# First head pair's queries and keys: loaded token by token in four transfers and turned by TensorE, instead of loaded in 32-column blocks by eight transfers and turned by VectorE

## The chip, the cores and the metric

The kernel runs on one core of one Trainium2 chip. The metric is the device time of one execution in microseconds. Before the change the median of three runs is 948.99 us (948.95 to 949.15).

## The reference: what is computed

Routing attention over 4 batches, 8 heads, 768 tokens and head size 64, followed by a feed-forward block on 3072 tokens. Each query and each key is assigned to one of 16 centroids of its head, and a query sees only the keys of its own cluster:

```python
q_assign = np.argmax(np.einsum('bhsd,hcd->bhsc', q_n, c_n), axis=-1)
k_assign = np.argmax(np.einsum('bhsd,hcd->bhsc', k_n, c_n), axis=-1)
mask = q_assign[:, :, :, None] == k_assign[:, :, None, :]
scores = np.where(mask, scale * np.matmul(q, k.transpose(0, 1, 3, 2)), -1e9)
attn = softmax(scores)
x = np.matmul(attn, v)
h = x @ w_in
g = h * erf(softplus(h))
out = g @ w_out
```

All inputs and the output are float32. The weights are 512 x 2048 and 2048 x 512.

## The kernel before, in words

The attention part works on 16 pairs of heads (one batch, two heads that lie on the two halves of the 128 partitions). For each pair it needs the queries and keys with the head dimension on the partitions and the 768 tokens along the free axis: `qT` and `kT`, 128 x 768 float32. From these it computes, in this order: the similarities to the 32 centroid columns of the two heads (`similarities`, four TensorE products into the bank `turned[1]`, one each for a half of the queries and a half of the keys); the choice of the best centroid (`choose`: a VectorE transposition `sims`, a maximum, a comparison `hot`, a transposition `hotT`); one-hot mask rows for queries and keys (`masks`, bf16 tiles `qm`, `km`); bf16 copies of queries and keys (`vectors`: ScalarE writes `qv`, `kv`); the maximum of each query's scores (`maxima_step`, six of them for a pair, into `nmx`); and then the scores, exponentials, sums and products with `v`, in periods that interleave one pair's attention with the next pair's preparation (`period`, and lines 1541 to 1543). The feed-forward part comes after all pairs.

The change touches the start of the program, where the first pair cannot hide behind another one.

**Loading.** `load` (line 221) brings queries or keys of a pair as four transfers each, one for a head and a block of 32 columns of the head dimension. The tile `in_q` or `in_k` is 128 x 24 x 32: partition `e*64 + g*32 + t` holds token `t` of each of 24 token blocks, with 32 columns of head `e`. A run of memory is 32 floats, 128 bytes, and a transfer of 96 KB has 768 of them. So `qT` comes out of one VectorE transposition of 32 x 32 blocks over 128 x 768. `load_qk(p)` (line 244) does both for pair `p`. Pair 0 and pairs from 2 on use the pool `stage`, which has one buffer a name; pair 1 uses the memory of `x_more` (line 167). Transfers go out on the list `queues` (line 216), SyncE and ScalarE; after pair 0's (line 256) both entries are SyncE's. Line 251 loads the centroids, lines 253 and 255 pair 0, line 257 pair 1, line 1501 pair 2; pair 0's `v` and the first blocks of the weight `w_in` follow on SyncE (lines 1524 to 1526).

**Order.** `te`, `ve`, `ae`, `ge` and `sy` are the five engines, wrapped so that each keeps the program's order (line 119). While the first loads are under way, TensorE executes products that nobody reads: `warm(n, into, rhs)` issues `n` bf16 products with the identity as the stationary operand. Before the change there are 17 of them on 256 columns (line 1487), then the transposition of the normalised centroids `cn` into `pct` (line 1489), then 3 more on 384 columns. VectorE normalises the centroids (lines 356 to 371; `twice` is an intermediate of the square root), then transposes `qT` (line 1493), copies the turned centroids into `ccT` (two copies, one for each half of the partitions), and transposes `kT` (line 1499). `similarities(0)`, `vectors(0, ...)`, `products(0)` (the first score products, into a `sc` buffer of the two in the pool `ps_s`) and `warm(9, ...)` follow, then `choose(0)`.

**Names of PSUM tiles.** `wide` has two banks, used here for the maxima; `also` is the other buffer of `ps_s` (line 1513), used in turn with `wide` by the six first maxima; `turned[0]` and `turned[1]` are one bank each. `HW` is 384, half of the tokens; `HJ` is 3, the 128-token tiles of a half.

Of the kernel before, what the change touches and what calls it, by code (L numbers as in the profile page):

```python
# [9 lines left out]
F32 = mybir.dt.float32  # L10
# [9 lines left out]
P = 128  # L20
B, H, S, D = 4, 8, 768, 64
C = 16
NJ = S // P
Q = 32
NB = S // Q
HW = S // 2
QW = HW // 2
TW = QW + 1
HJ = NJ // 2
# [106 lines left out]
def kernel(  # L136
# [13 lines left out]
    te, ve, ae, ge = (  # L150
        InOrder(tc, e, in_order) for e in (nc.tensor, nc.vector, nc.scalar, nc.gpsimd)
    )
# [8 lines left out]
    turned = [ps.tile([P, 512], F32, name=f"turned{i}") for i in range(2)]  # L161
# [5 lines left out]
    x_more = const.tile([P, 3, HK, HT], F32, name="x_more")  # L167
# [6 lines left out]
    def passing(name, bufs, **kw):  # L174
        return attention.enter_context(tc.tile_pool(name=name, bufs=bufs, **kw))

    ps_s = passing("ps_s", 2, space=PSUM)
    wide = passing("ps_w", 1, space=PSUM).tile([P, 2, 512], F32, name="wide")

    const = passing("fixed", 1)  # L180
    stage = passing("stage", 1)
# [4 lines left out]
    ident = const.tile([P, P], F32, name="ident")  # L186
    identb = const.tile([P, P], BF16, name="identb")
    first = const.tile([P, P], BF16, name="first")
    pick = const.tile([P, 2, P], BF16, name="pick")
# [18 lines left out]
    rows = [{nm: const.tile([P, S], F32, name=f"{nm}T{i}") for nm in "qk"} for i in range(2)]  # L208
# [5 lines left out]
    pairs = {}  # L214
    sy = InOrder(tc, nc.sync, in_order)
    queues = [sy, ae]

    def heads(p):
        return p // HP, 2 * (p % HP)

    def load(p, nm, src, pl):
        if p >= NPAIR:
            return
        b, h0 = heads(p)
        if nm == "v":
            t = pl.tile([P, NJ, 2, D], F32, name="in_v")
            for e in range(2):
                queues[0].dma_start(out=t[:, :, e], in_=src[b, h0 + e].rearrange("(j p) d -> p j d", p=P))
        else:

            if pl is None:
                t = x_more.rearrange("p a k t -> p (a k t)")[:, (nm == "k") * S : (1 + (nm == "k")) * S]
                t = t.rearrange("p (n t) -> p n t", t=Q)
            else:
                t = pl.tile([P, NB, Q], F32, name="in_" + nm)
            for e in range(2):
                for g in range(D // Q):
                    queues[e if nm == "q" else e * g].dma_start(
                        out=t[e * D + g * Q : e * D + (g + 1) * Q],
                        in_=src[b, h0 + e, :, g * Q : (g + 1) * Q].rearrange("(n t) d -> t n d", t=Q),  # L240
                    )
        pairs.setdefault(p, {})[nm] = t

    def load_qk(p):
        load(p, "q", q, stage if p != 1 else None)
        load(p, "k", k, stage if p != 1 else None)
# [3 lines left out]
    cen = setup[:, 0:D]  # L250
    sy.dma_start(out=cen, in_=centroids.rearrange("h c d -> (h c) d"))

    load(0, "q", q, stage)
    tc.keep_in_program_order(nc.scalar.preload_act_table_set("natural_log_exp_and_others"))
    load(0, "k", k, stage)
    queues[1] = sy
    load_qk(1)

    make_identity(nc, ident)
    ve.memset(ccT, 0.0)  # L260
# [4 lines left out]
    for base, pattern, sign, op, fill in (  # L265
# [5 lines left out]
            out=first, in_=first, compare_op=op, fill=fill, base=base, pattern=pattern,  # L271
# [78 lines left out]
    def scalar_tile():  # L350
        n = next(spare)
        return setup[:, n : n + 1]
# [10 lines left out]
    ve.reciprocal(out=inv, in_=norm)  # L363
    twice = scalar_tile()
    ve.scalar_tensor_tensor(out=twice, in0=ss, scalar=inv, in1=norm, op0=ALU.mult, op1=ALU.add)
    norm = scalar_tile()
    ve.tensor_scalar(out=norm, in0=twice, scalar1=0.5, scalar2=1e-6, op0=ALU.mult, op1=ALU.add)
    rden = scalar_tile()
# [164 lines left out]
    def products(u):  # L533
        p, half, j = units[u]
        if u in sc_of:
            return
        st = pairs[p]
        sc = sc_of[u] = ps_s.tile([P, 2, 512], F32, name="sc", tag="s")
        for e in range(2):
            r = slice(e * D, (e + 1) * D)  # L540
            te.matmul(
                sc[:, e, 0:HW], lhsT=st["kT"][r, j * P : (j + 1) * P],
                rhs=st["qT"][r, half * HW : (half + 1) * HW], start=True, stop=False,
            )
# [937 lines left out]
    def warm(n, bank, rhs):  # L1482
        for _ in range(n):
            te.matmul(bank[:, 0 : rhs.shape[-1]], lhsT=identb, rhs=rhs, start=True, stop=True)

    zeros = lowest[1].rearrange("p t n -> p (t n)")
    warm(17, turned[1], pick.rearrange("p h n -> p (h n)"))
    pct = turned[0][:, 0:P]
    te.transpose(out=pct, in_=cn.rearrange("p e d -> p (e d)"), identity=ident)
    warm(3, turned[1], zeros)  # L1490
    st = pairs[0]
    st["qT"], st["kT"] = rows[0]["q"], rows[0]["k"]
    ve.transpose(out=st["qT"], in_=st.pop("q").rearrange("p n t -> p (n t)"))
    for e in range(2):
        ve.tensor_copy(
            out=ccT[e * D : (e + 1) * D, :, e * C : (e + 1) * C],
            in_=pct[e * D : (e + 1) * D].rearrange("d (r e c) -> d r e c", e=2, c=C)[:, :, e],
        )
    ve.transpose(out=st["kT"], in_=st.pop("k").rearrange("p n t -> p (n t)"))
    st.update(lows[0])  # L1500
    load_qk(2)
    similarities(0)
# [2 lines left out]
    for r in (0, D):  # L1505
        for half in range(2):
            for e in range(2):
                c = r + half * Q + e * C
                ve.tensor_copy(
                    out=pick[r : r + D, half, e * D : (e + 1) * D].rearrange("p (n c) -> p n c", n=2)[:, :, 1 : C + 1],  # L1510
                    in_=first[r : r + D, c : c + C].unsqueeze(1).to_broadcast([D, 2, C]),
                )
    also = ps_s.tile([P, 2, 512], F32, name="sc", tag="s")
    products(0)
    warm(9, turned[0], zeros)
    run(choose(0))
# [132 lines left out]
```

## Time and profile before

| | |
|---|---|
| median of three runs | 948.99 us (948.95 to 949.15) |
| the profiled execution's own time | 948.84 us |
| its span, first to last instruction | 947.1 us |
| outside the span | 1.74 us |
| TensorE busy | 938.7 us, 99% of the span |
| VectorE busy | 783.4 us, 83% |
| ScalarE busy | 546.9 us, 58% |
| GpSimd busy | 505.3 us, 53% |

The engines are called PE (TensorE products), PEld (its weight loads), DVE (VectorE), ACT (ScalarE), POOL (GpSimd) and SP (SyncE); a `q` behind the name is the engine's sequencer, which waits and issues transfers. The **chain of waits** is followed back from the last instruction: at each step to what released it, or to the instruction before it on its engine; its rows are a start in us, a duration in us, and what ran. The **timeline** lists instructions in order of time, neighbours of one kind merged: start, duration of the merged stretch, engine, line, operation, what is written and read, sizes, count, and in brackets the engine's idle time before it and what ended it. The view of **groups** gives for each kind of instruction its count, the busy time and the mean of one in ns. The view of **transfers** gives, for a stretch of time, the packets that the transfer engines moved, and their rate. Nearly all instructions carry line 127, that of the wrapper, so rows are told apart by the tiles they name. A product's record includes its way through the array, so records of neighbouring products overlap; what one costs in a row of many is the distance between starts.

### The profile page before, as it was taken

To read this page: it belongs to the slowest core of one execution; us is meant where nothing else is said; L and a number is where in the kernel's file an instruction comes from. 1 tells how busy PE (TensorE), PEld (TensorE's weight loads), DVE (VectorE), ACT (ScalarE), POOL (GpSimd) and SP (SyncE) were. 2 spreads that over 40 slices of the span, in tenths; PEclk is the share of its full clock that TensorE was granted. 3 is DMA by queue.
4 is the path that set the end of the run, shared out by engine and by line. 5 is a ranking of instruction groups with operands and counts; after the bars stand their busy time and mean duration, and the time that the engine had idled before them with its cause. 6 is when DMAs were issued, how large, how long until landed. Compare 5 with 4: busy or idle time off the path is not lost.

```text
span 947.1 us, 22315 instructions
## 1 busy us (share of the span) xinstructions
PE 938.7 (99%) x8756; PEld 707.0 (75%) x8756; DVE 783.4 (83%) x1416; ACT 546.9 (58%) x809; POOL 505.3 (53%) x357
## 2 busy tenths in 40 slices
PE   8999999999999999999999999999999999999998
PEld 3555555555555555588888888998999899989987
DVE  8888888888888887869886688688868977897887
ACT  3777777777777776476523543653257236525541
POOL 2688888888888888899119111460063016103600
PEclk9999999999999999999999999999999999999999
DMA  9354454444443621133885247353454436343533
GB/s 211 78 114 113 112 113 112 111 113 111 113 113 67 157 58 36 26 120 125 214 244 229 89 122 213 110 179 111 157 165 136 133 118 207 116 151 123 158 111 111
DMA packets 176344, 123.17 MB, mean 130 GB/s; under 512 B 132592, under 2 KB 143344, under 8 KB 176240
## 3 DMA queue, kind: packets, MB, share of 16 engines
q1 hardware_dynamic: 171872, 116.34, 43.2%
q0 software_dynamic: 1872, 4.98, 3.0%
q8 instruction: 69, 1.13, 0.5%
q10 hardware_dynamic: 2496, 0.43, 0.2%
q14 instruction: 35, 0.29, 0.1%
HBM read 91.78 MB, written 23.33 MB: 122 GB/s over the span
## 4 chain that ended last, share of the span: by engine, by line
PE 97%; DVE 1%; POOL 1%; DMA 0%; SPq 0%; ACT 0%; issue 0%; DVEq 0%; POOLq 0%
PE bank L127 43%; PE turned L127 31%; PE sc L127 17%; PE wide L127 6%; POOL more_out L127 1%; DVE nmx L127 1%; DMA in_k<-in_k_dram 0%; SPq L127 0%; DVE kT L127 0%; ACT qm L127 0%; ACT pr L127 0%; DVE sims L127 0%; ACT km L127 0%; DVE hotT L127 0%; DVE wide L127 0%
## 5 line engine op out<-in xcount | busy, mean ns | idle before, releaser
L127 POOL TENSOR_TENSOR more_out<-more_out,pr 128x768 f32<-128x768 f32 x128 | 217.6, 1700 | 17.1 <-ACT pr L127 7.5
L127 DVE TENSOR_REDUCE nmx<-wide 128x2 f32<-128x512 f32 (+2 forms) x189 | 179.1, 948 | 47.1 <-PE wide L127 46.1
L127 ACT ACTIVATE pr<-sc 128x768 f32<-128x768 f32 x192 | 148.4, 810 | 81.1 <-PE wide L127 73.2
L127 PE MATMUL turned<-pr,in_v 128*32 128x193 f32 x3072 | 145.2, 330 | 0.0
L127 POOL TENSOR_TENSOR g<-g 128x512 f32<-128x512 f32 x36 | 47.1, 1308 | 180.8 <-DVE g L127 178.8
L127 PEld LDWEIGHTS turned<-pr,in_v 128*32 128x32 f32 x3072 | 90.2, 109 | 51.3 <-issue 26.9
L127 DVE TENSOR_TENSOR g<-g 128x512 f32<-128x512 f32 x132 | 90.7, 687 | 23.0 <-PE bank L127 12.2
L127 PE MATMUL sc<-qT,kT 64*128 64x384 f32 x528 | 98.5, 485 | 0.0
L127 DVE TENSOR_TENSOR g<-bank,g 128x256 f32<-128x256 f32 (+1 forms) x128 | 64.6, 531 | 18.3 <-PE bank L127 9.5
L127 PE MATMUL bank<-g_more,g 128*128 128x256 f32 x320 | 75.7, 379 | 0.0
L127 PE MATMUL bank<-x_own,w_in 128*128 128x128 f32 (+1 forms) x440 | 74.0, 309 | 0.0
L127 ACT ACTIVATE a_s<-g 128x1024 f32<-128x1024 f32 x38 | 39.6, 1055 | 58.7 <-POOL g L127 45.9
L127 POOL TENSOR_TENSOR more_out<-pr,pr 128x768 f32<-128x768 f32 x32 | 59.2, 1849 | 19.7 <-ACT pr L127 19.6
L127 PEld LDWEIGHTS bank<-g_more,g 128*128 128x128 f32 x320 | 60.7, 190 | 8.6 <-DVE g L127 0.3
L127 DVE TENSOR_TENSOR g<-a_s,g 128x512 f32<-128x512 f32 x76 | 66.2, 892 | 0.8 <-ACT a_s L127 0.8
L127 PEld LDWEIGHTS bank<-x_own,w_in 128*128 128x128 f32 x440 | 63.2, 191 | 4.4 <-issue 0.6
L127 PE MATMUL wide<-kv,qv 64*128 64x256 bf16 (+2 forms) x378 | 64.8, 327 | 0.9 <-ACT km L127 0.6
L127 PE MATMUL bank<-w_out,g 128*128 128x256 f32 x280 | 64.5, 379 | 0.0
L127 PEld LDWEIGHTS <-qv 64*128 64x128 bf16 x384 | 23.1, 93 | 52.7 <-issue 37.8
L127 PE MATMUL wide<-km,qm 64*128 64x256 bf16 (+4 forms) x378 | 62.2, 326 | 0.0
L127 ACT ACT_TABLE_LOAD x40 | 51.3, 1283 | 17.7 <-DVE g L127 17.1
L127 PEld LDWEIGHTS sc<-qT,kT 64*128 64x128 f32 x528 | 46.3, 187 | 19.0 <-issue 2.0
(240 smaller groups left out, 1988.0 us busy)
## 6 DMA issues: line engine op xcount, KB each, us to landing
g_more<-b_dram SPq DMA_DIRECT2D x52, 512.0 KB
g_more<-w_dram SPq DMA_DIRECT2D x84, 256.0 KB
x_own<-in_moe_w_in_dram SPq DMA_DIRECT2D x13, 512.0 KB
in_v<-in_v_dram SPq DMA_DIRECT2D x32, 192.0 KB
x_dram<-more_out SPq DMA_DIRECT2D x128, 48.0 KB
x_own<-x_dram SPq DMA_DIRECT2D x6, 1024.0 KB
in_k<-in_k_dram SPq DMA_DIRECT2D x59, 96.0 KB
in_q<-in_q_dram SPq DMA_DIRECT2D x58, 96.0 KB
```

Of the source, the lines that this page charges most:

```text
L127: ins = getattr(self.engine, name)(*args, **kw)
```

## The change

The first pair no longer goes through `load`. For queries and for keys, a tile of the same `stage` buffer is filled by two transfers, one a head: partition `p` holds the tokens `j*128 + p` for six values of `j`, each with 64 floats of head 0 and 64 of head 1. Head 0 goes out on SyncE, head 1 on ScalarE; a transfer has 192 KB in 768 runs of 256 bytes. Pair 1's loads move from line 257 to a place behind the VectorE instruction `twice`; a VectorE memset of one column of `x_more` stands ahead of them, which all of its query transfers overwrite, so that they wait for it.

The turning is done by TensorE: a 128 x 128 block (128 tokens by two heads' 64 columns) is a single transposition, six for the queries (into `wide`) and six for the keys (into `also`, which is now taken earlier). Four copies out of PSUM, each 128 x 384 float32, replace the two VectorE transpositions: ScalarE copies the first halves, VectorE the second halves. The 17 warming products become 8, and the 3 behind `pct` are gone; `pct` now stands between the two halves of the keys.

```diff
-    load(0, "q", q, stage)
+    lying = {}
+    for nm, src in (("q", q), ("k", k)):
+        t = stage.tile([P, NB, Q], F32, name="in_" + nm).rearrange("p n t -> p (n t)")
+        lying[nm] = t.rearrange("p (j e d) -> p j e d", e=2, d=D)
+        for e in range(2):
+            queues[e].dma_start(out=lying[nm][:, :, e], in_=src[0, e].rearrange("(j p) d -> p j d", p=P))
     tc.keep_in_program_order(nc.scalar.preload_act_table_set("natural_log_exp_and_others"))
-    load(0, "k", k, stage)
+    pairs[0] = {}
     queues[1] = sy
-    load_qk(1)
...
     ve.scalar_tensor_tensor(out=twice, in0=ss, scalar=inv, in1=norm, op0=ALU.mult, op1=ALU.add)
+    ve.memset(x_more[:, 0, 0, 0:1], 0.0)
+    load_qk(1)
...
-    warm(17, turned[1], pick.rearrange("p h n -> p (h n)"))
+    warm(8, turned[1], pick.rearrange("p h n -> p (h n)"))
+    also = ps_s.tile([P, 2, 512], F32, name="sc", tag="s")
+    st = pairs[0]
+    st["qT"], st["kT"] = rows[0]["q"], rows[0]["k"]
+
+    def turned_whole(nm, bank, half):
+        for n in range(HJ):
+            te.transpose(
+                out=bank[:, half, n * P : (n + 1) * P],
+                in_=lying[nm][:, half * HJ + n].rearrange("p e d -> p (e d)"), identity=ident,
+            )
+        return bank[:, half, 0:HW]
+
+    to_q = [turned_whole("q", wide, half) for half in range(2)]
+    to_k = [turned_whole("k", also, 0)]
     pct = turned[0][:, 0:P]
     te.transpose(out=pct, in_=cn.rearrange("p e d -> p (e d)"), identity=ident)
-    warm(3, turned[1], zeros)
-    st = pairs[0]
-    st["qT"], st["kT"] = rows[0]["q"], rows[0]["k"]
-    ve.transpose(out=st["qT"], in_=st.pop("q").rearrange("p n t -> p (n t)"))
+    to_k.append(turned_whole("k", also, 1))
+    ae.copy(out=st["qT"][:, 0:HW], in_=to_q[0])
+    ve.tensor_copy(out=st["qT"][:, HW:], in_=to_q[1])
+    ae.copy(out=st["kT"][:, 0:HW], in_=to_k[0])
     for e in range(2):
         ve.tensor_copy(
             out=ccT[e * D : (e + 1) * D, :, e * C : (e + 1) * C],
             in_=pct[e * D : (e + 1) * D].rearrange("d (r e c) -> d r e c", e=2, c=C)[:, :, e],
         )
-    ve.transpose(out=st["kT"], in_=st.pop("k").rearrange("p n t -> p (n t)"))
+    ve.tensor_copy(out=st["kT"][:, HW:], in_=to_k[1])
...
-    also = ps_s.tile([P, 2, 512], F32, name="sc", tag="s")
     products(0)
```

## The prediction

> **What bounds the kernel now.** I read first the page (which engine fills the span), then the chain of waits over the first 12 us, then the timeline of the same stretch, then the transfers.
>
> ```profile
> PE 938.7 (99%) x8756; PEld 707.0 (75%) x8756; DVE 783.4 (83%) x1416; ACT 546.9 (58%) x809; POOL 505.3 (53%) x357
> ...
> PE 97%; DVE 1%; POOL 1%; DMA 0%; SPq 0%; ACT 0%; issue 0%; DVEq 0%; POOLq 0%
> ```
>
> Over the whole span TensorE is the bound: it is busy 99% and makes 97% of the chain. What ends sooner ahead of that long stretch ends the program sooner by the same amount, unless something else is due there. The start is different:
>
> ```profile
> 2.28 0.53 SPq L127
> ...
> 3.42 3.21 DMA in_k<-in_k_dram
> 6.64 0.02 issue
> 6.66 0.99 DVE kT L127
> 7.65 0.04 issue
> 7.69 0.86 PE turned L127 x4
> 8.55 0.02 issue
> 8.58 0.59 DVE sims L127
> ...
> 11.40 0.59 ACT km L127
> ```
>
> SyncE issues one key transfer after the other, the last lands at 6.64, VectorE turns `kT`, TensorE makes the similarities, and `sims` starts at 8.58. From there to the mask rows at 11.40 the chain runs through choices and masks that the change leaves alone. So its worth is read at one place: when does `sims` start, 8.58 now? Round it the timeline has:
>
> ```profile
> 0.80 0.99 ACTq L127 DMA_DIRECT2D in_q<-in_q_dram  x2
> 1.26 0.98 SPq L127 DMA_DIRECT2D in_q<-in_q_dram  x2
> 2.28 2.13 SPq L127 DMA_DIRECT2D in_k<-in_k_dram  x3
> 2.40 3.50 PE L127 MATMUL turned<-pick,identb 128*128 128x256 bf16 x17 [2.40 <-DVE alleps L127]
> 3.94 0.22 DVE L127 SCALAR_TENSOR_TENSOR pr<-pr 128x1 f32<-128x1 f32 x1
> 4.45 2.55 SPq L127 DMA_DIRECT2D x_more<-in_q_dram  x4
> 4.58 0.42 DVE L127 TENSOR_SCALAR pr<-pr 128x64 f32<-128x64 f32 x2
> 5.18 0.98 DVE L127 STREAM_TRANSPOSE qT<-in_q 128x768 f32<-128x768 f32 x1 [0.18 <-DMA in_q<-in_q_dram]
> 5.74 0.27 PE L127 MATMUL turned<-ident,pr 128*128 128x128 f32 x1
> 5.85 0.65 PE L127 MATMUL turned<-lowest,identb 128*128 128x384 bf16 x3
> 6.08 0.43 DVE L127 COPY ccT<-turned 64x64 f32<-64x64 f32 x2
> 7.05 2.53 SPq L127 DMA_DIRECT2D x_more<-in_k_dram  x4
> 9.31 1.64 PE L127 MATMUL turned<-lowest,identb 128*128 128x384 bf16 x9
> 9.69 2.15 SPq L127 DMA_DIRECT2D in_q<-in_q_dram  x4
> 14.31 1.11 SPq L127 DMA_DIRECT2D in_v<-in_v_dram  x2
> 19.04 0.97 DVE L127 STREAM_TRANSPOSE qT<-x_more 128x768 f32<-128x768 f32 x1
> 24.03 1.51 PE L127 MATMUL turned<-pr,in_v 128*32 128x193 f32 x32
> ```
>
> **The loads.** Eight transfers of 96 KB become four of 192 KB, 0.79 MB both ways, with the centroids' 32 KB ahead. An issue takes about 0.53 us whether its 768 runs are short or long (the three `in_k` issues 2.13 us with a gap; the two `in_v` issues, of the new shape, 1.11). SyncE is then through by 1.26 + 1.06 = 2.3 us instead of 4.4, ScalarE by 1.8, so the transfer engines set the landing. Their busy tenths in 0.2 us slices from 0 to 8 us, and their rates between 2.0 and 5.4 us (128-byte runs, both queues), 16 to 17 us (256-byte runs, `v` of pair 0) and 25.2 to 26.4 us (`v` of pair 1):
>
> ```profile
> DMA  0000000005999999999999999999967999999999
> ...
> DMA packets 5455, 0.69 MB, mean 203 GB/s; under 512 B 5455, under 2 KB 5455, under 8 KB 5455
> ...
> DMA packets 1054, 0.26 MB, mean 263 GB/s; under 512 B 1054, under 2 KB 1054, under 8 KB 1054
> ...
> DMA packets 1012, 0.26 MB, mean 220 GB/s; under 512 B 1009, under 2 KB 1009, under 8 KB 1012
> ```
>
> Packets start in the tenth slice, about 1.1 us behind the first issue, at 1.9. Then 0.82 MB at 263 GB/s last 3.1 us: keys landed at 5.0, plus about 0.1 for the landing itself; at 220 GB/s 5.7; at today's 203 GB/s 6.05. I take 263, since 16 to 17 us is filled by such runs alone, while the other stretch runs out at its end. Queries go first on both queues, but ScalarE's queue has a start of 0.46 us and comes to its keys before SyncE's queries are through: half of the bytes and about half of that head start, so 3.8 to 4.2.
>
> **The turning on TensorE.** The eight warming products and then twelve transpositions stand in one row in program order. Their cost is the distance between starts:
>
> ```profile
> 4.94 0.74 PE L127 MATMUL turned<-pick,identb 128*128 128x256 bf16 x3
> ...
> 5.15 0.64 PE L127 MATMUL turned<-pick,identb 128*128 128x256 bf16 x3
> ...
> 5.37 0.54 PE L127 MATMUL turned<-pick,identb 128*128 128x256 bf16 x3
> ...
> 588.70 0.72 PE L127 MATMUL bank<-x_own,w_in 128*128 128x128 f32 x5
> ```
>
> Starts at 4.94, 5.15, 5.37 are 0.21 apart; the three from 5.37 are followed by the centroids' transposition at 5.74, 0.12 each. So TensorE doubles its speed near 5.45, some 3.05 us into its work; the granted clock in the windows shows 1.00 throughout and does not tell this. The existing transposition costs 0.11 (5.74 to 5.85) and is one product; a float32 row of such blocks at 588.70 costs (0.72 - 0.27) / 4 = 0.11 too. At the slow speed I take 0.21.
>
> Step by step: warming ends at 2.40 + 8 x 0.21 = 4.10, about when the queries land. Six turns at 0.21 run to 5.39, their last result out of the array at 5.6 (a record is 0.16 to 0.2 longer than its distance). The keys have landed by 5.1. If the speed doubles at 5.45 as now, the first three key turns run to 5.78, `pct` to 5.89 (result 6.05), the last three to 6.23, result 6.40.
>
> Here the Trainium skill speaks against the change. The row is the doubling near 5.45, 3.05 us after the first product. The page "TensorE: Matmul & The Clock Gate", Part 1, says that the gate opens after a busy window of about 3.4 us and that this window runs freely, so the opening moves from run to run. By the row the sum below stands; by the page an opening at 7.5 is as possible, which is rival 1's time. Whether the opening moves, no run here shows.
>
> **The copies.** Groups of the same size or neighbours in size, of the first 12 and 20 us:
>
> ```profile
> L127 DVE TENSOR_SCALAR qm<-wide 128x384 bf16<-128x384 f32 x1 | 0.6, 557 | 0.4 <-PE turned L127 0.4
> ...
> L127 ACT ACTIVATE qm<-turned 128x384 bf16<-128x384 f32 x1 | 0.5, 491 | 0.6 <-PE turned L127 0.6
> ```
>
> A VectorE copy is put at 0.55, a ScalarE one at 0.49. On VectorE, in order: second half of the queries 5.64 to 6.19; the two `ccT` copies, 0.43, 6.22 to 6.65 (`pct` is long there); second half of the keys 6.68 to 7.23. ScalarE's copies of the first halves, 5.0 to 5.5 and 6.0 to 6.5, lie in time when it idles, and end before VectorE's. So VectorE, not the loads, is now last: two transpositions of 0.98 become two copies of 0.55, but only the final one stands behind the last arrival.
>
> **The sum.** From the end of the last `kT` instruction to `sims` it is 8.58 - 7.65 = 0.93 us. 7.23 + 0.93 = 8.16, against 8.58: a gain of 0.42 us. Bounds: with the speed doubled from 4.1 on, turns and keys at 5.1 give 6.05 for the last result, 6.73 for the copy, `sims` at 7.66, gain 0.92; with keys landing at 6.05 the last result comes at 7.0, the copy ends at 7.65, gain 0.
>
> **What is moved.** Pair 1's eight transfers wait for a memset behind the instruction at 3.94; with 0.22 for that and about 0.1 for the memset, SyncE starts them at 4.3 instead of 4.45. The eight issues take 5.1 us today (4.45 to 9.58), so pair 2's, at 9.69 today, go out at 9.5 or sooner; in SyncE's order they pass nothing else. Their first reader is the transposition at 19.04, which shows no wait; `v` of pair 0, queued behind them, is issued at 14.31 and read at 24.03. If the gate held SyncE longer, these 5 to 10 us are the cover. The memset adds under 0.1 to the centroids, ready at 5.0 and read at 5.78; without that cover it would cost its 0.1. The bf16 copies `qv`, `kv` on ScalarE move by some tenths and are first read behind `km` at 12 us. Nothing else is near its due time, so the gain reaches the end of the program whole.
>
> **Rivals.** (1) *Nothing is won*: loads at today's 203 GB/s, or the doubling only behind the key turns, which then cost 0.21 each: last result 7.1, last copy to 7.7; `sims` at 8.6, 949.0 us. For it: the 220 row, and the 128-column turns with a weight load each, which may count as less work than the warming row. Against: 263 GB/s in a pure stretch. (2) *More is won*: speed doubled early; up to 0.92, 948.1. Against: the rows show 0.21 until 5.37. (3) *Slower: the array stays at half speed* because 1.7 us of warming instead of 3.5 is not enough, or because the queries land after 4.10 and leave a hole. It decides if the doubling comes later than about 7.7, where the last similarities start. Put one stretch of 3.05 us later, at 8.5: the copy ends at 7.7, the similarities (0.86 now) take 0.5 to 0.6 more, `sims` at 9.15: +0.6, 949.6. Two stretches, at 11.5: the first score products and the nine warming products at 9.31 (1.64 us now) also run at half speed and stand ahead of the masks, about +1.5, 950.5. Three, at 14.6: the first maxima's products too, an estimated +3.5, 952.5. Against: TensorE has no hole longer than a few tenths from 2.40 to 6.2. (4) *The holding back does not do what it says*: if pair 1's loads were not held at all, they would share the engines from 3.5 us and the keys would land near 6; that is rival 1's time. (5) *Something beyond these rows* wins over 1.9 us; no wait in the quoted stretch is that long once the keys have landed.
>
> **How the numbers follow.** The sum is made against the profiled execution: 947.1 of span and 1.74 outside are 948.84; 0.42 less is 948.42. The median of the runs is 0.15 above that execution, so the median forecast is 948.99 - 0.42 = 948.6. Chances: forecast (gain 0.2 to 0.6) 0.54; rival 1 with rival 4, 0.16; rival 2, 0.10; rival 3, 0.15, of which 0.10 beyond 950.9; rival 5, 0.05. A change of 0.2%, 1.9 us, is about what a measurement of this kernel can tell from none; by it faster is rival 5, slower the upper part of rival 3, and all else is within. The range 947.7 to 949.9 takes in both bounds of the loads and the first step of rival 3.
>
> **What would show it.** Right: warming ends near 4.10 and the query turns follow without a hole; keys landed by 5.1 and not waited for; starts 0.11 apart from about 5.45; the VectorE row copy, `ccT`, copy unbroken from 5.64; `sims` at 8.16; the transposition at 19.04 and all behind it 0.4 earlier. Wrong: turns that wait for a transfer, starts 0.21 apart behind 5.5, a SyncE queue that resumes late, or a shift at 20 us that differs from that of `sims`.

## The result, and the profile after

| | before | after |
|---|---|---|
| median | 948.95 us (948.91 to 949.15, 7 runs) | 952.18 us (951.85 to 953.12, 7 runs) |
| ratio | | 1.0036, 95% interval 1.0026 to 1.0046 |
| the profiled execution's own time | 948.84 us | 951.92 us |
| its span | 947.1 us | 950.2 us |

The change makes the kernel 3.2 us slower; 948.6 was predicted. The engines' line of the page after:

```profile
PE 939.8 (99%) x8756; PEld 708.1 (75%) x8756; DVE 782.9 (82%) x1417; ACT 547.4 (58%) x811; POOL 505.0 (53%) x357
```

TensorE is still the bound, so the loss must again be a shift. The chain of waits after, from the first query transfer to the similarities:

```profile
1.26 3.87 DMA in_q<-in_q_dram
5.13 0.14 issue
5.26 1.52 PE wide L127 x6
6.78 0.69 PE sc L127 x3
7.46 0.21 PE turned L127
7.68 0.64 PE sc L127 x3
8.32 0.08 issue
8.39 1.93 PE turned L127 x8
10.32 0.02 issue
10.35 0.59 DVE sims L127
```

`sims` starts at 10.35, where 8.16 was predicted and 8.58 stood before. The queries land at 5.13, a microsecond late; then the chain never leaves TensorE. The timeline of the same stretch shows why (the bracket is the engine's idle time before the row, and what ended it):

```profile
2.40 1.89 PE L127 MATMUL turned<-pick,identb 128*128 128x256 bf16 x8 [2.40 <-DVE alleps L127]
...
5.26 1.52 PE L127 MATMUL wide<-ident,in_q 128*128 128x128 f32 x6 [0.97 <-DMA in_q<-in_q_dram]
6.59 0.88 PE L127 MATMUL sc<-ident,in_k 128*128 128x128 f32 x3
6.81 0.48 ACT L127 COPY qT<-wide 128x384 f32<-128x384 f32 x1 [2.55 <-PE wide L127]
...
7.32 0.56 DVE L127 COPY qT<-wide 128x384 f32<-128x384 f32 x1 [1.77 <-ACT qT L127]
7.47 0.85 PE L127 MATMUL sc<-ident,in_k 128*128 128x128 f32 x3
...
8.35 0.48 ACT L127 COPY kT<-sc 128x384 f32<-128x384 f32 x1 [1.06 <-PE sc L127]
8.39 0.90 PE L127 MATMUL turned<-qT,ccT 128*32 128x384 f32 x4
...
8.86 0.56 DVE L127 COPY kT<-sc 128x384 f32<-128x384 f32 x1 [0.62 <-ACT kT L127]
...
10.35 0.58 DVE L127 STREAM_TRANSPOSE sims<-turned 128x384 f32<-128x384 f32 x1 [0.18 <-PE turned L127]
```

Three things stand in it. The array idles 0.97 us between the warming and the first turn. The six query turns start 6.59 - 5.26 = 1.33 us ahead of the first key turn, 0.22 each, which is half speed; the trace holds the moment at which the granted clock rises as a record of its own (no view of the profile lists it, and the windows' mean does not show it): 8.57, against 5.45 before. And the copies do not run side by side: ScalarE's copy of the first half starts at 6.81, behind all six turns, and VectorE's copy waits 1.77 us for ScalarE's, though the two write and read different halves.

The transfer engines between 2.0 and 6.5 us after (40 slices; busy tenths, rate in each):

```profile
DMA  4456999999999999999999999999999512789999
GB/s 98 102 137 146 212 289 289 291 289 267 278 280 285 289 289 282 237 230 230 223 225 221 228 210 221 214 225 182 203 173 171 89 30 46 121 139 156 192 173 161
DMA packets 4084, 0.91 MB, mean 203 GB/s; under 512 B 4084, under 2 KB 4084, under 8 KB 4084
```

They are half idle until 2.5 us, reach 290 GB/s for 1.2 us, and then fall to between 210 and 240. In the trace the keys land at 6.45, against 6.64 before: four transfers with runs twice as long won 0.2 us.

TensorE stands 1.78 us behind the execution of before at 25 us, as `sims` does (10.35 - 8.58 = 1.77), and stays between 1.75 and 1.95 up to 440 us. From 452 us it is 3.02 behind. So a second loss of 1.1 us lies where the diff has nothing. At 559 us 0.21 come back, as they do in the trace of kernel 4 below, a pure delay. Behind the last TensorE product there is one loss more: from its start to the last instruction of the program it is 3.98 us before and 4.22 after. VectorE near 440 us, before and then after:

```profile
437.13 0.42 DVE L127 TENSOR_TENSOR g<-bank,g 128x256 f32<-128x256 f32 x1
437.66 0.96 DVE L127 TENSOR_TENSOR g<-turned,g 128x256 f32<-128x256 f32 x2
...
440.05 0.72 DVE L127 TENSOR_TENSOR g<-a_s,g 128x512 f32<-128x512 f32 x1
```

```profile
439.01 0.42 DVE L127 TENSOR_TENSOR g<-bank,g 128x256 f32<-128x256 f32 x1
439.89 0.95 DVE L127 TENSOR_TENSOR g<-turned,g 128x256 f32<-128x256 f32 x2 [0.46 <-PE bank L127]
...
442.28 1.59 DVE L127 TENSOR_TENSOR g<-a_s,g 128x512 f32<-128x512 f32 x1
```

The same instruction starts 0.53 us behind its predecessor's start before, and 0.88 after: a pause of 0.35 us. The bracket names TensorE, but VectorE's wait for it ends at 439.50 in the trace after, 0.40 us ahead of the start; before, 0.04 us lie between the two. A little later an instruction on `a_s` and `g` takes 1.59 instead of 0.72 us: it now starts 0.22 us behind a GpSimd instruction (442.06 in the trace) instead of 0.14 ahead of it (440.19), and the time is not made up. The instruction that pauses has the place 834 in VectorE's program (834 stand ahead of it, its waits counted) before the change, and 831 after, since the change adds and removes VectorE instructions early on.

### The profile page after: what moved, and what is told of

It reads as the page before. It is cut to its first block, busy times and chain, and to the rows that moved or that the text cites. A ratio compares the mean times of both kernels' runs of the same rounds, so it can differ in the third digit from the quotient of the medians.

```text
span 950.2 us, 22312 instructions
## 1 busy us (share of the span) xinstructions
PE 939.8 (99%) x8756; PEld 708.1 (75%) x8756; DVE 782.9 (82%) x1417; ACT 547.4 (58%) x811; POOL 505.0 (53%) x357
## 3 DMA queue, kind: packets, MB, share of 16 engines
q8 instruction: 69, 1.13, 0.5%
## 4 chain that ended last, share of the span: by engine, by line
PE 96%; DVE 2%; issue 1%; DMA 1%; SPq 0%; ACT 0%; DVEq 0%
PE bank L127 42%; PE turned L127 31%; PE sc L127 17%; PE wide L127 6%; DVE g L127 1%; DVE nmx L127 1%; DMA in_q<-in_q_dram 0%; SPq L127 0%; DMA qm<-least_rows 0%; DVE g_more L127 0%; ACT qm L127 0%; DVE sims L127 0%; DVE hotT L127 0%; ACT km L127 0%; DVE wide L127 0%
```

## The experiments

The theory after the result had four parts: the loads land late and leave a hole in the warming; the hole keeps the clock gate, which holds TensorE at half speed, shut; the copies are put in a row because both engines read one PSUM tile; and the pause at 440 us belongs to the place in VectorE's program. The rivals are named in each expectation. Times are medians; "before" in the same runs was 948.89 to 948.96 throughout.

**1. The hole filled** (13 warming products, otherwise the kernel after).

```diff
-    warm(8, turned[1], pick.rearrange("p h n -> p (h n)"))
+    warm(13, turned[1], pick.rearrange("p h n -> p (h n)"))
```

> The changed kernel with 13 warming products instead of 8, so that TensorE has no hole between 4.29 and 5.26 us where it waits for the queries. Gate theory (the hole keeps TensorE at half speed until 8.57): starts of the key turns 0.11 apart, VectorE's sims at about 9.5 instead of 10.35, time 0.8 lower, about 951.3. Rival (the loads and the copies alone cost the time): turns still land as late, sims at 10.2 or later, time within 0.3 of 952.2.

Measured 951.48 us (951.01 to 951.91), ratio 1.0027 (1.0016 to 1.0038), `sims` at 9.53, the clock's change at 5.98. The hole is 0.7 us of the loss; the loss at 450 us stays.

**2. A PSUM tile of its own for each half** (four tiles instead of two, `pct` ahead of the keys; eight warming products).

```diff
-    to_q = [turned_whole("q", wide, half) for half in range(2)]
-    to_k = [turned_whole("k", also, 0)]
-    pct = turned[0][:, 0:P]
+    to_q = [turned_whole("q", (wide, also)[half][:, 0], half) for half in range(2)]
+    pct = also[:, 1, 0:P]
...
-    to_k.append(turned_whole("k", also, 1))
+    to_k = [turned_whole("k", turned[1 - half], half) for half in range(2)]
```

> The changed kernel with the four halves in four different PSUM tiles (first query half in wide, second in also, first key half in turned[1], second in turned[0], the centroids' turn in also ahead of the keys), so that ScalarE's and VectorE's copies have no tile in common. Copy theory (two engines that read one PSUM tile are put one after the other): VectorE's copy of the second key half starts right behind the last turn, at about 8.35 instead of 8.86, sims at about 9.85, time 0.5 lower, 951.7. Rival (the order comes from the destination tile, or costs nothing): sims stays at 10.3, 952.2. The gate still opens after 8 us in both.

**3. Both.** Kernel 2 with 13 warming products:

```diff
-    warm(8, turned[1], pick.rearrange("p h n -> p (h n)"))
+    warm(13, turned[1], pick.rearrange("p h n -> p (h n)"))
```

> Both: 13 warming products and four PSUM tiles. If the two costs are separate they add: sims at about 8.9, 0.3 behind the kernel before, and 1.4 us below the changed kernel, about 950.8. If the loads' late landing (keys 6.45) is what is left, nothing behind it waits longer than in the kernel before.

Kernel 2: 950.55 us (949.79 to 951.52), ratio 1.0018 (1.0008 to 1.0027). Its profiled execution is its slowest, with the clock's change at 11.26 and `sims` at 10.81, a microsecond behind what was expected. Its median is lower than expected, 951.7, because the loss at 450 us is missing: kernels 2 and 3 stand at place 832. What the tiles are worth is therefore read against kernel 5 below, which has that place too (951.05). Kernel 3: 950.11 us (949.71 to 950.59), ratio 1.0012 (1.0003 to 1.0021), `sims` at 9.28. Its timeline:

```profile
5.15 0.85 PE L127 MATMUL wide<-ident,in_q 128*128 128x128 f32 x3
5.79 0.83 PE L127 MATMUL sc<-ident,in_q 128*128 128x128 f32 x3
6.03 0.48 ACT L127 COPY qT<-wide 128x384 f32<-128x384 f32 x1 [1.79 <-PE wide L127]
...
6.77 0.56 DVE L127 COPY qT<-sc 128x384 f32<-128x384 f32 x1 [1.24 <-PE sc L127]
...
7.10 0.48 ACT L127 COPY kT<-turned 128x384 f32<-128x384 f32 x1 [0.58 <-PE turned L127]
7.25 0.45 DVE L127 COPY ccT<-sc 64x64 f32<-64x64 f32 x2
7.72 0.56 DVE L127 COPY kT<-turned 128x384 f32<-128x384 f32 x1
```

ScalarE's copy starts behind the three turns of its own half, and VectorE no longer waits for ScalarE: it was the shared tile. The wait that is gone was one for ScalarE's semaphore, that is a wait in the program; what the chip would do without it, no run shows.

**4. A delay alone** (the kernel before, 20 instead of 9 warming products ahead of the masks).

```diff
-    warm(9, turned[0], zeros)
+    warm(20, turned[0], zeros)
```

> The kernel before with 20 instead of 9 warming products ahead of the first masks, that is a pure delay of about 1.7 us at 11 us, and nothing else changed. If the changed kernel's second loss (about 0.9 us near 440 to 450 us) comes from the shift alone, this kernel has it too: 951.5 to 952. If it comes from something else in the change, the shift is carried as it is: 950.6 to 950.8.

950.66 us (950.6 to 950.93), ratio 1.0019 (1.0009 to 1.0028). TensorE is 2.2 us behind at 25 us and still at 440 and 452, and 2.0 from 559 us on: a delay at the start is carried on nearly whole, and does not bring the loss at 450 us.

**5 and 6. The place in VectorE's program.** The kernel after with one VectorE memset more; and the kernel before with four VectorE memsets moved to GpSimd, so that the place is 831 as after.

```diff
+    ve.memset(ccT[:, 0, 0:1], 0.0)
```

```diff
-        ve.memset(t, FLOOR)
+        ge.memset(t, FLOOR)
...
-    ve.memset(minus, -1.0)
-    ve.memset(alleps, S * EPS)
+    ge.memset(minus, -1.0)
+    ge.memset(alleps, S * EPS)
```

> The changed kernel with one more VectorE instruction at the start (a one-column memset of a tile that is zero already, 0.06 us, in a stretch where VectorE waits for the centroids). Theory: the second loss near 440 us starts with a pause of 0.35 us ahead of one VectorE instruction that stands 831 places from the start of VectorE's stream in the two kernels that lose (the changed one and the one with 13 warming products) and 832 or 834 places in the four that do not; one instruction more moves it to 832, the pause goes, and so does the loss: 951.1 to 951.3. Rival (a lottery of VectorE's and GpSimd's phases that depends on the start): 952.2 as the changed kernel.

> The kernel before with four of VectorE's memsets at the start done by GpSimd (and one wait more), so that the same VectorE instruction stands 831 places from the start of its stream instead of 834. Nothing on the early path changes. Place theory: the pause of 0.35 us and the loss of about 1 us near 440 us appear in the kernel before: 949.9 to 950.1. Rival: 948.95 as before.

The added instruction makes the kernel faster: 951.05 us (950.73 to 951.87) against 952.18. The kernel before, with nothing of the change, becomes slower: 950.12 us (949.68 to 950.28), ratio 1.0011 (1.0002 to 1.0021). VectorE in the latter:

```profile
437.28 0.42 DVE L127 TENSOR_TENSOR g<-bank,g 128x256 f32<-128x256 f32 x1
438.16 0.95 DVE L127 TENSOR_TENSOR g<-turned,g 128x256 f32<-128x256 f32 x2 [0.46 <-PE bank L127]
...
440.55 1.59 DVE L127 TENSOR_TENSOR g<-a_s,g 128x512 f32<-128x512 f32 x1
```

The same instruction pauses, and the same 1.59 us follow. So the loss at 450 us comes with the place, and needs nothing else of the change.

**7. One queue for the four transfers** (all on SyncE; one execution).

```diff
-            queues[e].dma_start(out=lying[nm][:, :, e], in_=src[0, e].rearrange("(j p) d -> p j d", p=P))
+            queues[0].dma_start(out=lying[nm][:, :, e], in_=src[0, e].rearrange("(j p) d -> p j d", p=P))
```

> The changed kernel with all four transfers of the first pair issued by SyncE, none by ScalarE. Theory that the two queues' packets are mixed, so that the queries finish only with half of the keys: queries now landed at about 4.5 instead of 5.13, keys at 6.4 as before. Rival (the shape itself is slow, about 0.19 MB a us, whatever the queue): queries at 5 or later too. Only the landings are looked at.

953.65 us. The queries landed at 5.56, the keys at 7.86, both later than with two queues, so the theory of the mixed queues is not borne out. It is no clean test of it: SyncE issues the keys at 2.30 and 2.89 us here, and the two queues issue them at 1.30 and 1.72.

**8. Holding pair 1 back, alone** (the kernel before with `load_qk(1)` behind `twice` and the memset).

```diff
-    load_qk(1)
...
+    ve.memset(x_more[:, 0, 0, 0:1], 0.0)
+    load_qk(1)
```

> The kernel before with one part of the change alone: pair 1's loads behind the memset. If pair 1's packets delay the first keys (issued from 4.45 on, moving from about 5.5), the keys land by 6.4 instead of 6.64 and the time falls by 0.2, 948.75. If not, 948.95. If the holding back itself costs (SyncE resumes late), over 949.2.

948.93 us (948.54 to 949.15), ratio 0.9999 (0.999 to 1.0009): nothing, either way. Pair 1's first load goes out at 4.45 us in it, as in the kernel before, so it shows that the memset costs nothing; what pair 1's packets do to the keys it does not test.

**9. Half of the bytes** (kernel 2 with half of the loads).

```diff
-            queues[e].dma_start(out=lying[nm][:, :, e], in_=src[0, e].rearrange("(j p) d -> p j d", p=P))
+            queues[e].dma_start(out=lying[nm][:, 0:HJ, e], in_=src[0, e, 0:HW].rearrange("(j p) d -> p j d", p=P))
...
-                in_=lying[nm][:, half * HJ + n].rearrange("p e d -> p (e d)"), identity=ident,
+                in_=lying[nm][:, n].rearrange("p e d -> p (e d)"), identity=ident,
```

> The kernel with four separate PSUM tiles and eight warming products, but only the first half of the tokens of the first pair's queries and keys is loaded (384 of 768 a head, the same three blocks turned twice), so half of these tokens is left out and replaced by the other half. It asks what the turning and the copies are worth when the data land as early as the prediction had them. If the landing, and the hole that it leaves in the warming, is the step of the prediction that failed: queries landed by about 4.3, keys by 5.2, no hole in TensorE's row beyond 0.3 us, sims starts at 8.2 to 8.7, and the time is 948.6 to 949.3. Rival, that the work behind the landing (copies, VectorE's train) costs the time wherever the data are: sims at 9.3 or later and 949.9 or more.

**10. The centroids' copies on ScalarE** (kernel 3, with `pct` in the second bank of `wide`; two early memsets keep the place).

```diff
+    ve.memset(ccT[:, 0, 0:1], 0.0)
+    ve.memset(ccT[:, 0, 0:1], 0.0)
...
-    pct = also[:, 1, 0:P]
+    ae.copy(out=st["qT"][:, 0:HW], in_=to_q[0])
+    pct = wide[:, 1, 0:P]
...
-    ae.copy(out=st["qT"][:, 0:HW], in_=to_q[0])
...
-    ae.copy(out=st["kT"][:, 0:HW], in_=to_k[0])
...
-        ve.tensor_copy(
+        ae.copy(
             out=ccT[e * D : (e + 1) * D, :, e * C : (e + 1) * C],
...
+    ae.copy(out=st["kT"][:, 0:HW], in_=to_k[0])
```

> The kernel with separate PSUM tiles and 13 warming products, with the two copies of the turned centroids moved from VectorE to ScalarE, so that VectorE has only the second halves of queries and keys to copy. (Two early memsets of a column that is written again keep VectorE's later instructions at the places that they have in the kernel compared with.) Theory, VectorE's train of copies stands behind the last turns: sims 0.3 to 0.4 earlier than 9.28, about 8.9, and 949.8 against 950.1. Rival, the keys' landing and the turns alone set it: sims at 9.2 to 9.3, 950.1, no change.

**11. The hole alone** (the kernel before).

```diff
-    warm(17, turned[1], pick.rearrange("p h n -> p (h n)"))
+    warm(8, turned[1], pick.rearrange("p h n -> p (h n)"))
```

> The kernel before with only 8 of its 17 warming products ahead of the centroids' transposition, and nothing else changed: a hole in TensorE's row from about 4.1 to 5.7 without any of the change's loads, turns or copies. Theory, the hole moves the opening of the clock gate (doubling of speed later than 7.5) and a part of the loss is this alone: 949.3 to 949.8 with a wider spread than the kernel before. Rival, the hole costs nothing by itself, the loss was in the loads and the copies: 948.95 within 0.2.

Kernel 9: the trace has the queries at 3.6 and the keys at 4.47, TensorE goes from the warming to the turns without a hole, and `sims` starts at 8.22, 0.06 from the predicted 8.16:

```profile
4.08 0.85 PE L127 MATMUL wide<-ident,in_q 128*128 128x128 f32 x3
...
8.22 0.58 DVE L127 STREAM_TRANSPOSE sims<-turned 128x384 f32<-128x384 f32 x1 [0.26 <-ACT kv L127]
```

Yet the time is 949.14 us (948.78 to 949.91), ratio 1.0004 (0.9994 to 1.0013): the 0.36 us gained at `sims` are 0.13 at 25 us. That became a question of its own (13 to 15). Kernel 10: 949.94 us (949.72 to 950.82), ratio 1.0012 (1.0003 to 1.0022), 0.17 below kernel 3, which such medians do not separate. `sims` was at 9.48 and not at 8.9: the keys landed at 6.75 in this execution, against 6.29. Counted from the landing it is 2.73 against 2.99 us. Kernel 11: 949.54 us (948.94 to 950.39), ratio 1.0009 (1.0000 to 1.0019), as its theory had it, and a spread of 1.45 us where the kernel before has 0.84 in the same runs. Its timeline has the hole, and behind it the slow array:

```profile
2.40 1.89 PE L127 MATMUL turned<-pick,identb 128*128 128x256 bf16 x8 [2.40 <-DVE alleps L127]
...
5.34 0.45 PE L127 MATMUL turned<-ident,pr 128*128 128x128 f32 x1 [1.04 <-DVE pr L127]
...
6.68 1.49 PE L127 MATMUL turned<-qT,ccT 128*32 128x384 f32 x4
```

**12. Pair 1's loads held until the queries are copied** (kernel 10).

```diff
-    ve.memset(x_more[:, 0, 0, 0:1], 0.0)
-    load_qk(1)
...
     ve.tensor_copy(out=st["qT"][:, HW:], in_=to_q[1])
+    ve.memset(x_more[:, 0, 0, 0:1], 0.0)
+    load_qk(1)
```

> The kernel with separate PSUM tiles, 13 warming products and the centroids' copies on ScalarE, with one edit: the memset that holds pair 1's loads back, and these loads, stand behind VectorE's copy of the queries instead of early in the centroids' chain, so that they are issued from about 7.3 instead of 4.4 and none of their packets runs while the first pair's keys are still under way. Theory, these packets took the transfer engines from the keys: keys landed at 5.8 to 6.2 instead of 6.75, sims at 8.7 to 9.1 instead of 9.48, and 949.3 to 949.7 against 949.94. If that is also enough to make up for the longer work behind the landing, it would be at 948.9 or less, which needs sims at 8.5 or sooner. Rival, the first pair's short runs are slow by themselves: keys landed at 6.4 to 6.8, sims at 9.2 to 9.5, and 949.9 or, if pair 1's later loads are missed further on, more.

949.83 us (949.55 to 950.46), ratio 1.0011 (1.0002 to 1.0020). At the place in question the theory held: keys landed at 6.10 instead of 6.75, `sims` at 8.89. But of the 0.59 us won there, still 0.58 at 65 us, 0.28 are left at 72 us. Near 69 us kernel 12 loses 0.42 us, the kernel after and kernel 15 (below) 0.13 to 0.14, and the kernels 4, 6, 8, 11 and 13, made from the kernel before, nothing; why was not tried. Kernel 12 is also not the best that these parts allow: the turn of the centroids goes into `wide`, waits there for ScalarE's copy of the queries (kernels 10 and 15 have the same wait) and starts at 6.31, and the key turns behind it start at 6.47, 0.37 us after the landing. An order without that wait was not run. The transfer engines from 2.0 to 6.2 us, with nothing but the first pair under way:

```profile
DMA  7689999999999999999999999999998443000000
GB/s 164 154 195 222 219 280 266 224 229 280 280 283 288 293 285 285 285 288 276 241 241 224 212 224 207 227 217 217 219 176 139 78 66 49 10 0 0 0 0 0
```

The last packets run at 5.6, and the landing is 0.45 us behind them. The fall from 285 to 220 GB/s near 4 us is there as well, so it is not pair 1's doing.

**13 to 15. The place again.** In the traces, all kernels at place 832 lost 0.22 to 0.23 us near 22 us, where VectorE's `sims` of pair 1 waited 0.57 instead of 0.17 us. Kernel 13 is the kernel before with two memsets moved (place 832); 14 is kernel 9, and 15 kernel 12, with two more early memsets (place 834).

```diff
-    ve.memset(minus, -1.0)
-    ve.memset(alleps, S * EPS)
+    ge.memset(minus, -1.0)
+    ge.memset(alleps, S * EPS)
```

```diff
+    ve.memset(ccT[:, 0, 0:1], 0.0)
+    ve.memset(ccT[:, 0, 0:1], 0.0)
```

> The kernel before with two of VectorE's early memsets (minus, alleps) moved to GpSimd, so that VectorE's later instructions stand two places earlier (832 instead of 834 for the one that paused at 831), and nothing of the change. Theory, the place alone costs the 0.23 us near 22 us: pair 1's similarities wait 0.57 instead of 0.17 us, the shift of TensorE grows by 0.2 to 0.25 there, no loss near 450 us, and the time is 949.1 to 949.3. Rival, the wait comes from the turned queries and keys: 0.17 as before, and 948.95.

> The half-loaded kernel (384 of 768 tokens of the first pair's queries and keys are loaded and turned twice, the others left out) with two more early memsets on VectorE, so that its later instructions stand where they stand in the kernel before. Theory, the place took the gain: sims at 8.2 to 8.4, pair 1's similarities wait 0.17, the shift stays at -0.2 to -0.35 from 8 us to the end, and 948.6 to 948.9, the prediction's sum with the prediction's landing. Rival, the gain is lost at pair 1 for another reason: the wait is 0.57 again and 949.1.

> The whole change with separate PSUM tiles, 13 warming products, the centroids' copies on ScalarE, pair 1's loads held until the queries are copied, and two more early memsets on VectorE for the place of before. Theory: sims at 8.8 to 9.1, pair 1's similarities wait 0.17, and 949.5 to 949.65 against 949.83, that is still 0.5 to 0.7 above before, the longer work behind the landing. Rival, with all of this put right the change wins: 948.9 or less.

Pair 1's `sims` before, in kernel 13 and in kernel 14:

```profile
21.88 0.58 DVE L127 STREAM_TRANSPOSE sims<-turned 128x384 f32<-128x384 f32 x1 [0.17 <-PE turned L127]
```

```profile
22.58 0.58 DVE L127 STREAM_TRANSPOSE sims<-turned 128x384 f32<-128x384 f32 x1 [0.57 <-PE wide L127]
```

```profile
21.72 0.58 DVE L127 STREAM_TRANSPOSE sims<-turned 128x384 f32<-128x384 f32 x1 [0.17 <-PE turned L127]
```

The kernel before shows the pause when two instructions are taken out ahead of it, and TensorE's shift grows by 0.22 us there (949.17 us, 948.8 to 949.53, ratio 1.0002, 0.9993 to 1.0011). Kernel 14 does not pause: 948.76 us (948.53 to 949.23), ratio 0.9999 (0.9991 to 1.0008), 0.19 below before and 0.38 below kernel 9, the former less than such medians separate; in its profile the clock rises at 6.39 and `sims` starts at 8.41. Kernel 15: 949.67 us (949.31 to 950.46), ratio 1.0010 (1.0001 to 1.0019), just above what was expected; its profiled execution, 950.34, had the clock's change at 8.24 and so `sims` at 9.93. No version that loads all tokens is faster than the kernel before.

## Why the prediction was wrong

The sum had `sims` at 8.16 and it came at 10.35, 2.19 us later. Against the kernel before `sims` is 1.77 us later and the profiled execution 3.08, so 1.3 us more are lost behind `sims`. Step by step, up to `sims`:

| step | predicted | after | off by |
|---|---|---|---|
| first query turn | 4.10 | 5.26 | 1.16 |
| from it to the last key turn's result | 2.30 | 8.32 - 5.26 = 3.06 | 0.76 |
| from there to the end of VectorE's key copy | 0.83 | 9.42 - 8.32 = 1.10 | 0.27 |
| from there to `sims` | 0.93 | 10.35 - 9.42 = 0.93 | 0 |

**The loads** are the step that failed first. The prediction took the rate of the best stretch of such runs, 263 GB/s, from a start at 1.9 us, and 0.1 us for the landing. The engines were half idle until 2.5, passed 263 for 1.2 us only, and the landing stood 0.45 us behind the last packet (kernel 12). With pair 1's loads out of the way, 0.82 MB from 1.9 to 5.6 us are 220 GB/s, the middle one of the prediction's three rates, and with the lag the keys land at 6.10, where it had its worst bound (6.05). In the kernel after, pair 1's packets run before the keys have landed and make it 6.45. So the holding back did too little: pair 1's issues began at 4.77, when the keys still had 1.7 us to go (rival 4 in part). The profiles agree: the earlier pair 1's first load goes out, the later the keys land, 6.91 for an issue at 4.23 (kernel 2), 6.75 for 4.40 (10), 6.29 to 6.45 for 4.74 to 4.82 (after, 1, 3 and 5), and 6.10 and 6.12 where it goes out behind them (12 and 15). That the queries would be there at 3.8 to 4.2 failed with it (5.13), since half of the bytes is not half of the time behind a slow start.

**The turning.** "Warming ends at 4.10, about when the queries land" left no margin: a landing one microsecond later made the hole. This is rival 3's condition, stated there as a doubling later than 7.7, and it had a chance of 0.15; the change of the clock came at 8.57 and all 12 turns cost 0.21. That turns may count as less work for the clock than the warming, rival 1's doubt, is not borne out: in kernel 15 it rises at 8.24, and from 5.15 on TensorE had executed nothing but turns. Filling the hole gave 0.7 us (kernel 1) and 0.44 (2 to 3), and the hole alone costs the kernel before 0.65 (11), with more spread. Rival 3's price, 949.6 for an opening at 8.5, was too low because it kept the early landing and the parallel copies, and had no loss behind `sims`.

**The copies.** "ScalarE's copies lie in time when it idles, and end before VectorE's" took them as parallel because they touch different halves. Kernels 2 and 3 show that the PSUM tile, not the half, sets the wait; separate tiles give 0.5 us (951.05 to 950.55). The quoted rows of single copies, 0.49 and 0.55, were right (0.48 and 0.56).

**What was right.** The tail from the copy to `sims` (0.93), the turn's cost at either speed, that nothing waits for the moved loads (the shift stays at 1.78 us from `sims` to 40 us), and the sum up to `sims` when the data are there: kernel 9 has it at 8.22. It is a match under better conditions than forecast: half of the bytes, a tile for each half, and keys landed at 4.47, ahead of the predicted 5.1. Kernel 14 takes 948.76 against the forecast of 948.6, with about half of the forecast gain. The prediction had the work behind the keys' landing longer by 8.16 - 5.1 = 3.06 against 8.58 - 6.64 = 1.94 us; it needed a landing 1.1 us earlier to break even, and got 0.2. In the best version, kernel 12's profile, it is 8.89 - 6.10 = 2.79, still 0.85 more than before, for a landing 0.54 earlier. That, with what is lost behind `sims`, is why none wins.

**"The gain reaches the end of the program whole"** failed in its unstated part, that some 940 us of unchanged instructions run unchanged. A delay is carried nearly whole (kernel 4), but a place three lower in VectorE's program costs 1.1 us at 440 us (5 and 6), and one two lower 0.22 at 22 us (13). And the change costs 0.24 us at the program's end, which the experiments did not take apart: from the last product's start to the last instruction all ten kernels with four transfers for the first pair take 4.21 to 4.23 us, the seven with eight 3.98 or 3.99. In the traces SyncE passes its last ten waits for transfers in a fixed order. Before, six of them are over by 1.6 us behind that product's start, and the last outputs land later; after, only two are, and the other four follow the landing at 0.06 each. That the number of transfers decides which waits come first is read from the traces; no run varied it alone.

Put together from the medians: place 831, 1.13 (after to kernel 5); copies in a row 0.50 (5 to 2); hole 0.44 (2 to 3); the centroids' copies 0.17 (3 to 10), pair 1's packets 0.11 (10 to 12), place 832 again 0.16 (12 to 15); and 0.72 (15 to before). The sum is 3.23. Of the 0.72, 0.24 lie behind the last product and 0.13 at 69 us, by kernel 15's trace; about 0.35 are left for the longer work behind the landing, an estimate that kernel 12's `sims`, 8.89 - 8.58 = 0.31 late, bears out. The steps below 0.3 us rest on the profiles named, not on their medians.

## What to carry to other kernels

A load's landing is worked out from the slowest comparable stretch, with its start and the lag behind its last packet, and work that must be unbroken behind it needs a margin of that size: here one microsecond late cost another 0.4 to 0.7 through the array's clock. Before two engines are counted as parallel, look whether they share a tile, not only whether they share bytes. And when instructions are added or removed ahead of a long stretch, compare the shift at several later times: a loss that begins where the diff has nothing can be the place in an engine's program, and one idle memset tells. Compare the stretch behind the last product as well.

## What the runs showed of the hardware

**The clock gate moves from run to run, and a hole of one microsecond moves it far.** Where the products behind the warming follow it without a hole, the trace records the rise of the clock between 5.34 (kernel 12) and 8.42 us (kernel 4), in 12 profiles; with a hole of 0.9 to 1.4 us it came between 8.27 (kernel 11) and 11.97 (kernel 7), in five. The prediction left open whether the opening moves; it does. The Trainium skill, page "TensorE: Matmul & The Clock Gate", Part 1, says that the gate opens after a busy window of about 3.4 us and that this window runs freely. The traces agree with the free-running window: the stretch at full clock lasts 942.08 us in 11 of the 17 profiles and 938.67 in six, 3.41 apart, and the openings without a hole are spread over 3.1 us. The page's spread of 0.5 us either way is less than that. Of the prediction's two readings, the row's (the doubling comes at 5.45 again) and the page's (7.5 as possible), the page's held.

**A pause that belongs to a place in VectorE's program.** It is 0.35 to 0.40 us long, at the instruction near 440 us in four kernels at place 831 (after, 1, 6 and 7), and at pair 1's `sims` in all kernels at place 832; kernels at place 834, and kernel 8 at 835, show neither. The two instructions that pause have 63 and 831 others ahead of them, and 831 is 12 x 64 + 63. The traces have more pauses at such places: 0.25 to 0.35 us at 1215 and 1343, each again 63 more than a multiple of 64, the kernel before among them (at 619.5 and 685.1 us), while the same instructions do not pause in kernels where they stand at other places. So place 834 is not free of pauses, it has them elsewhere; at most such places none shows. What the pause is stays open. Its price depends on what is behind it: 0.22 us in one case, 1.1 in the other, where the 1.59 us followed.

**Runs of 256 bytes** moved at 280 to 290 GB/s for a little over a microsecond and then at 210 to 230 with all 16 engines busy, also with no loads but the first pair's under way (kernel 12). Why they slow down was not tried.
